# Gated attention with a hash-routed expert layer: blocks of three sizes, gating of two groups on TensorE, u loads on another queue

## The chip, the cores and the metric

One core of one Trainium2 chip runs the whole program. The metric is the device time of one execution in microseconds. The kernel before was timed three times; the median counts. Engines are named as the profile names them: PE (TensorE matmul), PEld (its weight loads), DVE (VectorE), ACT (ScalarE), POOL (GpSimd), SP (SyncE).

## What is computed

Attention without softmax, multiplied by a gate, and then a layer of 8 experts in which an integer hash of the token's id picks the one expert of each token. All in fp32.

```python
# u, v: (8, 2496, 256)   z: (8, 2496, 64)
scores = (1.0 / S) * np.matmul(z, z.transpose(0, 2, 1))
attn = np.maximum(scores, 0.0) ** 2
x = (u * np.matmul(attn, v)).reshape(8 * 2496, 256)
# w1: (8, 256, 1024)   w2: (8, 1024, 256)
expert_idx = token_ids * np.int64(2654435761) % np.int64(8)
for e in range(8):
    m = expert_idx == e
    out[m] = np.maximum(x[m] @ w1[e], 0.0) @ w2[e]
```

## The kernel before

The program has two stages that TensorE goes through one after the other, attention and experts. The order of the work on every engine is the order in which the code emits it: a manual schedule is entered before the first load and left at the end, so what stands first on an engine's queue is done first, and an instruction that waits holds up all behind it on the same engine or DMA queue. Tiles rotate through pools of fixed numbers of buffers.

*Products.* Both stages multiply 2x2 block matrices with seven block products in place of eight (a Winograd form). It costs sums of blocks on VectorE: in attention `sums` (L258, four subtractions on the scores, L261 to L264) and `join` (L313, ACT copy L320 and DVE L322 to L328, which read the accumulators); in the experts the subtractions in `turn_x` and four operations on the hidden blocks (L912 to L915). The generator `products` (L860) emits one of the seven products at each `next`, in the order 1, 6, 7, 5, 2, 3, 4, and the operations that combine them behind them: L864 (ACT copy), L866, L871, L872, and L879 and L882 for the last ones. Product 3 accumulates into the PSUM bank of product 5, which L872 reads first.

*Attention.* Eight batches, each with five groups of queries `g`, each with five steps over keys: 200 steps. A step takes scores on TensorE (`score`, product L228), squares and clips them on ACT and DVE (L242 to L250), takes sums, and accumulates on TensorE (`attend`, L301, product L310). Scores are symmetric, so some are turned by DVE (L272), kept in HBM (L281) and read back (L289). z is read in pieces, turned by DVE (L171) from `zn` tiles. The group's last step is followed by `join`.

*Gating and sorting.* The joined outputs `o` have queries along the free dimension. For all groups but the last, `gate` (L330) turns them on DVE, `put` (L347) writes them to HBM, `fetch` (L353) reads them back by rows into `x_row` and loads u (`load_u`, L202, issued on SP's queue, L206), `multiply` (L370, DVE L374) multiplies by u, and `sort` (L390, GpSimd's indirect DMA L395) scatters the rows to the slots of their experts in HBM. For the last group `gate_late` (L376) turns the outputs by TensorE with an identity (L384), multiplies straight from PSUM (L386) and sorts; it is spread over the first expert step.

*Routing.* A generator (L415 to L604), advanced once per attention step from the sixth on, computes each token's expert and slot. In it DVE counts the tokens (`have`, L488), and after a `yield` a small matmul (L492) adds the counts over partitions. Another generator prepares sums of weights in HBM (`prepare`, L627, sums L644 and L645).

*Experts.* The slots form blocks of one expert each: NL=32 large ones of 512 slots and NR=35 small ones of 128, which hold what large ones leave. A large block goes through `load_x` (L679, SP), `turn_x` (L686, DVE transposes L697, subtractions L702 to L705), `up_large` (L886; product L901 of 4 instructions of 256 columns; 7 products in each of two halves of the hidden width), ACT activations L908, and `down_large` (L917; product L931 of 16 instructions of 128 columns). A small block uses plain products, `up_small` (L946, L954, 32 instructions of 128 columns) and `down_small` (L962, L965, 16 of 256 columns). `store` (L852, L854) scatters the output rows by GpSimd. `load_w` (L712) loads the weights of a block on SP (L717, L720, L724).

The loop L989 has one step for each large block: up products of block i, down products of block i−1, and the turning of block i+1, interleaved by the string ORDER (L976): U and u are up products of a large and a small block, D and d down products, X and x parts of `turn_x`, G parts of `gate_late`. SMALL (L982) spreads the small blocks over the steps, one or two in each. After its step, the x of the blocks of step i+2 and their weights are loaded on SP's queue. The first two blocks are "SURE": their x is loaded ahead, and turned in the last two attention steps.

Of the kernel before, what the change touches and what calls it, by code (L numbers as in the profile page):

```python
# [25 lines left out]
def kernel(  # L26
# [26 lines left out]
    BLK = 512  # L53
    TB = BLK // P
    NL = -(-(N - E * (BLK - 1)) // BLK)
    NR = (N - NL * BLK + E * (P - 1)) // P
    NB = NL + NR
    NS = NL * TB + NR

# [142 lines left out]
    def load_u(b, g, home=None):  # L202
        u_sb[b, g] = (home or rowpool).tile([P, 2, 2, D], F32, name="u_sb")
        for t in range(2):
            n = keys(g, t)
            nc.sync.dma_start(out=u_sb[b, g][0:n, :, t],  # L206
                              in_=uf[ds(b * S, S), :].rearrange("(q s) d -> s q d", q=2)[ds(g * W + t * P, n)])
# [105 lines left out]
    def join(g, acc, home):  # L313

        w = queries(g)
        p = {m: acc[k][:, half, 0:w] for m, (k, half) in BANK.items()}
        o = home.tile([P, DP, 2, W], F32, name="o")
        r = opool.tile([P, 2, W], F32, name="r", bufs=1)
        p1, u2 = r[:, 0, 0:w], r[:, 1, 0:w]
        nc.scalar.copy(p1, p[1])  # L320
        c = lambda i, q: o[:, i, q, 0:w]
        nc.vector.tensor_add(c(0, 0), p1, p[2])  # L322
        nc.vector.tensor_add(u2, p1, p[6])
        nc.vector.tensor_add(c(0, 1), u2, p[5])
        nc.vector.tensor_add(c(0, 1), c(0, 1), p[3])
        nc.vector.tensor_add(u2, u2, p[7])
        nc.vector.tensor_add(c(1, 1), u2, p[5])
        nc.vector.tensor_sub(c(1, 0), u2, p[4])  # L328
        return o
# [46 lines left out]
    def gate_late(b, g, o):  # L376

        x_sb = late.tile([P, 2, 2, D], F32, name="x_row")
        for q in range(2):
            ps = down_ps.tile([P, 2, D], F32, name="g_ps", tag="any")  # L380
            for t in range(2):
                m = keys(g, t)
                for i in range(DP):
                    nc.tensor.transpose(ps[0:m, t, ts(i, P)], o[:, i, q, ds(t * P, m)], ident[:])  # L384
                x, y = times_u(b, g, x_sb, q, t, m)
                nc.vector.tensor_mul(x, ps[0:m, t].rearrange("p (h i k) -> p i h k", h=DP, k=L), y)  # L386
                sort(b, g, x_sb, 2 * q + t)
            yield
# [26 lines left out]
    def places():  # L415

        with tc.tile_pool(name="route", bufs=1) as route:
# [31 lines left out]
            def fill():  # L449
                if unfilled:  # L450
# [3 lines left out]
                        x_dram[ds(NL * BLK + c * P, n * P), :].rearrange("(c p) d -> p c d", p=P), zero[:].unsqueeze(1).to_broadcast([P, n, D]))  # L454
# [35 lines left out]
            yield  # L490
# [23 lines left out]
            upto = wpool.tile([P, E, C], F32, name="upto", tag="w")  # L514
# [10 lines left out]
            nc.vector.tensor_tensor_scan(upto[:].rearrange(flat_e), one[:].to_broadcast([P, E * C]), upto[:].rearrange(flat_e), 0.0,  # L525
                                         op0=OP.mult, op1=OP.add)
            yield
            nc.vector.tensor_add(rank[:], rank[:], upto[:])
# [21 lines left out]

            large, large_end = share(count, BLK, 0, NL, "large")
            in_large = route.tile([P, E], F32)
            nc.vector.tensor_scalar(in_large[:], large[:], float(BLK), None, op0=OP.mult)
            nc.vector.tensor_sub(count[:], count[:], in_large[:])
            small, small_end = share(count, P, P - 1, NR, "small")

            shift = route.tile([P, E], F32)
            nc.vector.tensor_sub(shift[:], large_end[:], large[:])  # L560
            nc.vector.scalar_tensor_tensor(shift[:], shift[:], float(BLK), first[:], op0=OP.mult, op1=OP.subtract)
            more = route.tile([P, E], F32)
            nc.vector.tensor_sub(more[:], small_end[:], small[:])
            nc.vector.tensor_scalar(more[:], more[:], float(P), float(NL * BLK), op0=OP.mult, op1=OP.add)
            nc.vector.tensor_add(first[:], first[:], in_large[:])
            nc.vector.tensor_sub(more[:], more[:], first[:])
            nc.vector.tensor_sub(more[:], more[:], shift[:])

            for end, b0, nb in ((large_end, 0, NL), (small_end, NL, NR)):
# [4 lines left out]
                eb = route.tile([1, max(NL, NR)], F32, name="eb")  # L576
# [9 lines left out]
            past = upto  # L586
            nc.vector.tensor_tensor(past[:], rank[:], each(first), op=OP.is_ge)
            yield
            nc.vector.tensor_mul(past[:], past[:], each(more))
            yield  # L590
            nc.vector.tensor_add(rank[:], rank[:], each(shift))
            yield
            nc.vector.tensor_add(rank[:], rank[:], past[:])
            yield
# [78 lines left out]
    def large(j):  # L673
        return j < NL

    def slot_tiles(j):
        return range(j * TB, (j + 1) * TB) if large(j) else range(NL * (TB - 1) + j, NL * (TB - 1) + j + 1)

    def load_x(j):  # L679
        n = len(slot_tiles(j)) * P  # L680
        xq[j] = gpool.tile([P, n // L, DP, L], F32, name="xq" if large(j) else "xqs")
# [4 lines left out]
    def turn_x(j):  # L686

        n = len(slot_tiles(j))
        if large(j):
            x = gpool.tile([P, 2, DP, 2 * P], F32, name="xT")  # L690
            t = gpool.tile([P, 4, 2 * P], F32, name="xs")
        else:
            x, t = gpool.tile([P, 1, DP, P], F32, name="xTs"), None
        xT[j] = x, t
        m = min(2, n) * P // L
# [12 lines left out]
    def turn_x_at_once(j):  # L708
        for _ in turn_x(j):
            pass  # L710

    def load_w(j, m):  # L712

        e = nc.sync.value_load(eb_i[0:1, j:j + 1], min_val=0, max_val=E - 1)
        if large(j):
# [13 lines left out]
    order.__enter__()  # L729

# [42 lines left out]
    for i, (b, g, s) in enumerate(steps):  # L773
# [14 lines left out]
        if i >= len(steps) - SURE:  # L788
            turn_x_at_once(i - len(steps) + SURE)
        if pos == NT - 1:  # L790
            done = (b, g, join(g, acc, opool if i < len(steps) - 1 else late))
# [8 lines left out]
        if pos == 0 and done is not None:  # L800
# [19 lines left out]
        elif is_routed:  # L820
# [6 lines left out]
            if len(fetched) < 2 and waiting and (len(waiting) > 1 or i > put_at + (1 if i < len(steps) - NT else 0)):  # L827
# [9 lines left out]
        if i == len(steps) - 2:  # L837
            load_u(b, g, late)
            load_w(1, 0)
# [46 lines left out]
    def up_large(j):  # L886
# [3 lines left out]
        h = hpool.tile([P, 2, 2, FQ, 2 * P], F32, name="h")  # L890
        sums = hpool.tile([P, 3, FQ, 2 * P], F32, name="hs")
        hid[j] = h, sums
        take = {1: (0, y11), 2: (2, y21), 3: (6, y22), 4: (3, t4), 5: (4, t1), 6: (5, t2), 7: (1, t3)}
        for f in range(0, FQ, 2):
            def made(m, ps):
                first = ps is None
                if first:
                    ps = up_ps.tile([P, 2, 2 * P], F32, name="h_ps", tag="held" if m in (1, 5) else "other")
# [5 lines left out]
            r = rpool.tile([P, 2, 2, 2 * P], F32, name="r")  # L904
# [12 lines left out]
    def down_large(j):  # L917
        h, sums = hid[j]
        x11, x12, x21, x22 = (h[:, k, i] for i in range(2) for k in range(2))
# [3 lines left out]
        def made(m, ps):  # L923
            first = ps is None
            if first:
                held = m in (1, 5)
                ps = down_ps.tile([P, 2, P], F32, name="o_ps", tag="held" if held else "other", bufs=2 if held else 1)
            x, k = take[m]
            for t in range(2):
# [4 lines left out]
        r = rpool.tile([P, 2, 2, P], F32, name="ro")  # L934
        o = rpool.tile([P, TB, D], F32, name="o_sb")
        c = lambda i, k: o[:, ts(i, 2), ts(k, P)]

        def done(x, i, k, ps=None):
            if ps is not None:
                nc.scalar.copy(x, ps)  # L940
            elif i != k:
                for t in (2 * i, 2 * i + 1):
# [19 lines left out]
    def down_small(j):  # L962
        ps = down_ps.tile([P, D], F32, name="o_ps", tag="any")
        for f in range(FP):
# [10 lines left out]

    ORDER = {"": "UuUDUuUDUdUDU" "XUDXUDUxUDUUDU", "made": "UuUDUuUDUdUDU" "XUDXuUDUxuUDUUDU",  # L976
             "next": "UuUDUuUDUdUDU" "XUDXUDUxUDUUxDU", "last": "UdUDUuUDUuUDU" "XUDXUDdUxUDUUDU",
             "first": "UUUUGUUGUUUUUUUU", "second": "DUDUUDUUDUUDUU" "xXUuDUXUuDUxUU"}
# [3 lines left out]
    SMALL = [range(0)] + [range(*(NL + (k * NR + NL // 2) // (NL - 1) for k in (i, i + 1))) for i in range(NL - 1)]  # L982
    assert all(1 <= len(x) <= 2 for x in SMALL[1:]) and max(len(x) for x in SMALL[1:4]) == 1 and SMALL[-1][-1] == NB - 1

    def at(i):

        return [i, *SMALL[i]] if 0 <= i < NL else []

    for i in range(NL + 1):  # L989
        parts = {}  # L990
        for j in at(i):
            parts.setdefault("U" if large(j) else "u", []).append((up_large if large(j) else up_small)(j))
        for j in at(i - 1):
            parts.setdefault("D" if large(j) else "d", []).append((down_large if large(j) else down_small)(j))
        for j in at(i + 1):
            if j >= SURE:
                parts.setdefault("X" if large(j) else "x", []).append(turn_x(j))
        if i == 0:
            parts = {"U": parts["U"], "G": [gate_late(*done)]}
        if i == 1:  # L1000
            parts["x"].insert(0, turn_x(SMALL[1][0]))
        parts = {p: chain(*x) for p, x in parts.items()}
        for p in ORDER["first" if i == 0 else "second" if i == 1 else next((k for k, n in (("made", i), ("next", i + 1), ("last", i - 1)) if len(at(n)) > 2), "")]:
# [3 lines left out]
        if i == 0:  # L1007
            closing["late"].close()
            w2pool = pool("w2pool", 2, reuse_waits="tile")
            load_w(0, 1)  # L1010
            for j in SMALL[1]:
                load_w(j, 0)
                load_x(j)
        for j in at(i + 2):
            load_x(j)
        for m in range(2):
            for j in at(i + 2 - m)[:2]:
                load_w(j, m)
        for m in range(2):
            for j in at(i + 2 - m)[2:]:  # L1020
# [31 lines left out]
```

## Time and profile before

| what | value |
|---|---|
| runs, us | 2515.74, 2511.03, 2512.28; median 2512.28 |
| profiled execution, us | 2507.8 |
| its span from first to last instruction, us | 2506.0 |
| granted TensorE clock, mean | 0.998 |
| ACT activations of scores, L242 | 508, 248.1 us in all |
| products L310 | 42% of the chain that ended last |
| products L931, L901, L228, L954, L965 | 16%, 15%, 8%, 5%, 5% of that chain |
| DMA moved | 557.19 MB, mean 222 GB/s |
| w loads, 1792 KB each, to landing | 11.3 us |
| u loads, 256 KB a group, to landing | 5.2 us |

All times are of one profiled execution, except the runs. A timeline line gives start, duration, engine, code line, operation, written and read tiles with their shape, and how many instructions are taken together; in brackets stands how long the engine idled before it and what released it. A line of waits gives engine, tile and line that waited, what for, then total, number of times and longest. A line of windows gives a stretch, its length, and busy time (number of instructions) of PE, PEld, DVE, ACT and POOL, then the granted clock, the share of the DMA engines and GB/s. [...]

### The profile page before, as it was taken

The numbers are of one execution on the slowest core, as the hardware profiler recorded it, in microseconds if no ns is written. First come the engines' busy times: TensorE is split into PE (matmuls) and PEld (weight loads), VectorE is DVE, ScalarE is ACT, GpSimd is POOL, SyncE is SP. The second block draws the span as 40 slices with busy tenths as digits, with TensorE's granted clock in tenths as the row PEclk, the third lists the DMA queues.
The fourth block names the chain that finished last, engine by engine and source line by source line (L and its number), as shares of the span: only waits on it lengthen the run. The fifth ranks groups of instructions, "written<-read, shape, count | busy, mean of one in ns | idle before, by whom it ended". The sixth has DMA issues, their size and how long they took to land.

```text
span 2506.0 us, 36968 instructions
## 1 busy us (share of the span) xinstructions
PE 2476.4 (99%) x13631; PEld 2110.9 (84%) x13631; DVE 1653.4 (66%) x3151; ACT 705.8 (28%) x1203; POOL 548.9 (22%) x532
## 2 busy tenths in 40 slices
PE   8999999999999999999999989999999999999998
PEld 6787787787787777877787889999999999999998
DVE  7798768768778677687687665545555555555553
ACT  4324324224223233133233112222222222222221
POOL 0000333322332233233223221111111111111112
PEclk9999999999999999999999999999999999999999
DMA  8776899798797897897888797766676667667762
GB/s 148 201 206 176 244 272 227 211 248 203 234 262 191 244 249 184 251 250 198 246 244 230 200 284 240 244 227 227 236 236 203 222 225 232 204 224 245 236 217 72
DMA packets 604661, 557.19 MB, mean 222 GB/s; under 512 B 287068, under 2 KB 544685, under 8 KB 594240
## 3 DMA queue, kind: packets, MB, share of 16 engines
q1 hardware_dynamic: 513984, 369.74, 54.6%
q10 hardware_dynamic: 63168, 97.86, 11.9%
q0 software_dynamic: 27328, 87.23, 10.0%
q8 instruction: 107, 1.75, 0.3%
q14 instruction: 74, 0.61, 0.1%
HBM read 375.55 MB, written 175.60 MB: 220 GB/s over the span
## 4 chain that ended last, share of the span: by engine, by line
PE 91%; DMA 5%; DVE 2%; issue 1%; SPq 0%; ACT 0%; POOL 0%; POOLq 0%; DVEq 0%; ACTq 0%
PE acc L310 42%; PE o_ps L931 16%; PE h_ps L901 15%; PE s_ps L228 8%; PE h_ps L954 5%; PE o_ps L965 5%; DMA a<-scores 3%; DMA u_sb<-in_u_dram 1%; DMA scores<-mirror 0%; DMA zn<-in_z_dram 0%; DVE x_row L374 0%; DVE t L261 0%; DVE t L262 0%; DVE t L263 0%; ACT a L242 0%
## 5 line engine op out<-in xcount | busy, mean ns | idle before, releaser
L242 ACT ACTIVATE a<-s_ps 128x512 f32<-128x512 f32 (+2 forms) x508 | 248.1, 579 | 736.5 <-PE s_ps L228 697.5
L310 PE MATMUL acc<-t,vc 128*128 128x256 f32 (+3 forms) x1600 | 402.6, 374 | 0.0
L310 PEld LDWEIGHTS acc<-a,v_sb 128*128 128x128 f32 (+1 forms) x1600 | 293.3, 190 | 125.0 <-issue 45.5
L310 PE MATMUL acc<-a,v_sb 128*128 128x256 f32 (+3 forms) x1600 | 382.6, 382 | 5.3 <-DVE o L322 5.2
L395 POOL DMA_INDIRECT x_slots<-x_row,row x160 | 192.3, 1202 | 849.7 <-DVE x_row L374 642.9
L310 PE MATMUL acc<-t,v_sb 128*128 128x256 f32 (+3 forms) x1600 | 369.7, 373 | 0.0
L310 PEld LDWEIGHTS acc<-t,vc 128*128 128x128 f32 (+1 forms) x1600 | 303.0, 190 | 34.5
L310 PEld LDWEIGHTS acc<-t,v_sb 128*128 128x128 f32 (+1 forms) x1600 | 303.5, 190 | 33.6
L261 DVE TENSOR_TENSOR t<-a 128x512 f32<-128x512 f32 (+1 forms) x200 | 134.5, 672 | 226.5 <-ACT a L250 162.0
L901 PE MATMUL h_ps<-xs,w 128*128 128x256 f32 x1024 | 258.1, 380 | 0.0
L931 PEld LDWEIGHTS o_ps<-w,h 128*128 128x128 f32 x2048 | 248.6, 192 | 6.5
L228 PE MATMUL s_ps<-zT 64*128 64x512 f32 (+1 forms) x960 | 241.4, 617 | 9.1 <-DVE zT L171 8.4
L931 PE MATMUL o_ps<-w,h 128*128 128x128 f32 x2048 | 249.3, 275 | 0.0
L908 ACT ACTIVATE h<-h 128x512 f32<-128x512 f32 x192 | 121.0, 630 | 349.1 <-DVE h L872 153.2
L854 POOL DMA_INDIRECT out_dram<-o_sb,idx x128 | 126.7, 990 | 420.8 <-ACT h L908 271.2
L272 DVE STREAM_TRANSPOSE mirror<-a 128x512 f32<-128x512 f32 x320 | 198.4, 677 | 6.6 <-DMA scores<-mirror 6.5
L310 PE MATMUL acc<-a,vc 128*128 128x256 f32 (+3 forms) x800 | 201.1, 374 | 0.0
L901 PE MATMUL h_ps<-xT,w 128*128 128x256 f32 x768 | 194.0, 382 | 1.2 <-DVE h L872 1.2
L901 PEld LDWEIGHTS h_ps<-xs,w 128*128 128x128 f32 x1024 | 178.5, 191 | 15.5
L931 PEld LDWEIGHTS o_ps<-w,hs 128*128 128x128 f32 x1536 | 186.4, 192 | 4.8
L931 PE MATMUL o_ps<-w,hs 128*128 128x128 f32 x1536 | 187.1, 275 | 0.0
L611 POOL DMA_INDIRECT slot_tokens<-token,addr x160 | 169.7, 1061 | 49.0 <-issue 48.1
(154 smaller groups left out, 2756.7 us busy)
## 6 DMA issues: line engine op xcount, KB each, us to landing
w<-w_blocks SPq DMA_DIRECT2D x64, 1792.0 KB, 11.3
scores<-mirror SPq DMA_DIRECT2D x276, 256.0 KB, 4.8
a<-scores ACTq DMA_DIRECT2D x48, 1024.0 KB, 5.8
w1s<-in_moe_w_dram SPq DMA_DIRECT2D x35, 1024.0 KB, 10.3
w2s<-in_moe_w_dram SPq DMA_DIRECT2D x35, 1024.0 KB, 11.5
a<-scores ACTq DMA_DIRECT2D x32, 896.0 KB, 7.3
w_blocks<-w POOLq DMA_DIRECT2D x16, 1792.0 KB, 8.1
u_sb<-in_u_dram SPq DMA_DIRECT2D x72, 256.0 KB, 5.2
```

The lines of the kernel that those rows point to most:

```text
L228: nc.tensor.matmul(to, z_h[:, ds(h * HS + s * W + j * P, P)], at, start=True, stop=True)
L242: nc.scalar.activation(to, at, AF.Relu, scale=1.0 / S)
L261: nc.vector.tensor_sub(t1, y12, y11)
L272: nc.vector.transpose(m[:, :, j, h].rearrange("p (n i) k -> p i n k", i=QB), a[:, j, h].rearrange("p (i t) q r -> p i (t q) r", t=2))
L310: nc.tensor.matmul(acc[k][:, half, 0:w], x[0:n, j, :], y[0:n, j], start=(first and j == 0 and half == 0), stop=(last and j == 1), skip_gro ...
L395: st = nc.gpsimd.indirect_dma_start(out=x_dram[:, :], out_offset=bass.IndirectOffsetOnAxis(ap=row[0:m, c:c + 1], axis=0), in_=x_sb[0:m, q, ...
L611: st = nc.gpsimd.indirect_dma_start(out=slot_dram[:, None], out_offset=bass.IndirectOffsetOnAxis(ap=addr[0:n, to:to + 1], axis=0), in_=tok ...
L854: st = nc.gpsimd.indirect_dma_start(out=out[:], out_offset=bass.IndirectOffsetOnAxis(ap=idx[:, col:col + 1], axis=0), in_=o, in_offset=Non ...
L901: nc.tensor.matmul(ps[:, r], w1[j][:, k, ts(f + r, P)], y, start=first and r == 0, stop=True, skip_group_check=True)
L931: nc.tensor.matmul(ps[:, t], x[:, f, ts(t, P)], w2_block(w2[j], k)[:, f], start=first and t == 0 and f == 0, stop=f == FQ - 1, skip_group_ ...
L954: nc.tensor.matmul(ps[:, i, :], w1[j][:, c, ts(f + i, P)], x[:, 0, c, 0:P], start=(c == 0), stop=(c == DP - 1))
L965: nc.tensor.matmul(ps[:], hid[j][:, f], w2[j][:, f, :], start=(f == 0), stop=(f == FP - 1))
```

## The change

1. Blocks come in three sizes: NL=32 of 512, NM=7 of 256 (mid), NR=21 of 128. Mid blocks use the seven products with operands of half the size (`up_big`, `down_big`), so their up products have 4 instructions of 128 columns and their down products 8. They stand at positions 4, 9, 14, 19, 24, 29 and 34 of 39 big blocks. A step has at most one small block; seven of them are put into the step after a mid, the others into other steps. The step loop has 39 steps and an end of down products with the last small one last.
2. Routing computes shares for three sizes, with one more comparison and multiplication on VectorE; the `yield` between `have` and the count matmul is gone.
3. `load_u` issues on GpSimd's queue. The last group's u is loaded four attention steps before the end, that of the group before it (group 3) in that group's last step.
4. The outputs of group 3 of the last batch, like those of the last group, are turned by TensorE and multiplied from PSUM (`gate_at_once`), in the fourth step from the end; they don't go through HBM.
5. In the first expert step both halves of the last group are turned behind the fourth up product into the two "held" banks of `down_ps`; multiplications and sorts are emitted behind all fourteen up products.
6. The two SURE blocks are turned one attention step earlier.
7. Twelve products of the identity with itself stand first on TensorE.

```diff
-            nc.sync.dma_start(out=u_sb[b, g][0:n, :, t],
+            nc.gpsimd.dma_start(out=u_sb[b, g][0:n, :, t],
...
-    def gate_late(b, g, o):
-        x_sb = late.tile([P, 2, 2, D], F32, name="x_row")
+    def gate_at_once(b, g, o, x_sb, bank):
+        made = []
         for q in range(2):
-            ps = down_ps.tile([P, 2, D], F32, name="g_ps", tag="any")
+            made.append(bank())
+            for t in range(2):
+                for i in range(DP):
+                    nc.tensor.transpose(made[q][0:keys(g, t), t, ts(i, P)], o[:, i, q, ds(t * P, keys(g, t))], ident[:])
+        yield
+        for q in range(2):
             for t in range(2):
                 m = keys(g, t)
-                for i in range(DP):
-                    nc.tensor.transpose(ps[0:m, t, ts(i, P)], o[:, i, q, ds(t * P, m)], ident[:])
                 x, y = times_u(b, g, x_sb, q, t, m)
-                nc.vector.tensor_mul(x, ps[0:m, t].rearrange("p (h i k) -> p i h k", h=DP, k=L), y)
-                sort(b, g, x_sb, 2 * q + t)
-            yield
+                nc.vector.tensor_mul(x, made[q][0:m, t].rearrange("p (h i k) -> p i h k", h=DP, k=L), y)
...
                 nc.vector.tensor_reduce(have[:], mask[:], axis=AX.X, op=OP.add)
             fill()
-            yield
             ps = mm_ps.tile([P, E], F32, name="cnt_ps", tag="mm")
             nc.tensor.matmul(ps[:], all1[:], have[:], start=True, stop=True)
...
+    warm = mm_ps.tile([P, P], F32, name="warm", tag="mm")
+    for _ in range(12):
+        nc.tensor.matmul(warm[:], ident[:], ident[:], start=True, stop=True)
...
-        if i >= len(steps) - SURE:
-            turn_x_at_once(i - len(steps) + SURE)
+        if i == len(steps) - 4:
+            x_sb = rowpool.tile([P, 2, 2, D], F32, name="x_row", bufs=3)
+            for _ in gate_at_once(*done, x_sb, lambda: mm_ps.tile([P, 2, D], F32, name="g_ps", tag="mm")):
+                pass
+            to_sort += [(*done[:2], x_sb, k) for k in range(4)]
+        if 0 <= i - (len(steps) - 3) < SURE:
+            for _ in turn_x(i - (len(steps) - 3)):
+                pass
...
         if i == len(steps) - 2:
-            load_u(b, g, late)
             load_w(1, 0)
+        if i == len(steps) - NT - 1:
+            load_u(b, g)
+        if i == len(steps) - 4:
+            load_u(b, g, late)
...
-    def up_large(j):
+    def up_big(j):
+        n = half(j)
-        h = hpool.tile([P, 2, 2, FQ, 2 * P], F32, name="h")
+        h = hpool.tile([P, 2, 2, FQ, 2 * P], F32, name="h")[:, :, :, :, 0:n]
...
-    def down_large(j):
+    def down_big(j):
+        n = half(j) // P
-            for t in range(2):
+            for t in range(n):
...
-    ORDER = {"": "UuUDUuUDUdUDU" "XUDXUDUxUDUUDU", "made": "UuUDUuUDUdUDU" "XUDXuUDUxuUDUUDU",
-             "next": "UuUDUuUDUdUDU" "XUDXUDUxUDUUxDU", "last": "UdUDUuUDUuUDU" "XUDXUDdUxUDUUDU",
-             "first": "UUUUGUUGUUUUUUUU", "second": "DUDUUDUUDUUDUU" "xXUuDUXUuDUxUU"}
+    ORDER = {"first": "UUUUGUUUUUUUUUU", "second": "DUDUDUUDUUDUU" "XUxUDUXUDUUUU",
+             "other": "UuUDUuUDUdUDU" "XUDXUDUxUDUUDU", "end": "DDDDDDDd"}
...
+    for i in range(NBIG):
+        BIG.append(mid.pop(0) if i % (NBIG // NM) == NBIG // NM - 1 and mid else large.pop(0))
+        SMALL.append([])
+    for behind in (True, False):
+        for i in range(NBIG - 1, 1, -1):
+            if small and BIG[i] < NL and (BIG[i - 1] >= NL) == behind and (behind or i % 2 == 0 or len(small) == 1):
+                SMALL[i].append(small.pop())
...
+            parts["G"] = gate_at_once(*done, x_sb, lambda: down_ps.tile([P, 2, D], F32, name="g_ps", tag="held", bufs=2))
...
         if i == 0:
+            for k in range(4):
+                sort(*done[:2], x_sb, k)
```

## The prediction, made before the changed kernel ran

> **What bounds the kernel now.** I read the page's busy times first, then what TensorE waits for, then windows and timelines around each edit.
>
> ```profile
> PE 2476.4 (99%) x13631; PEld 2110.9 (84%) x13631; DVE 1653.4 (66%) x3151; ACT 705.8 (28%) x1203; POOL 548.9 (22%) x532
> ...
> PE s_ps L228 <- DVE zT L171: 8.4, 2, 7.3
> PE g_ps L384 <- DVE x_row L386: 5.6, 2, 4.7
> PE acc L310 <- DVE o L322: 5.2, 7, 1.9
> PE h_ps L901 <- DVE h L872: 1.2, 1, 1.2
> ...
> 1520.00:2480.00 960.00, 960.00 (x6562) 903.52 (x6561) 508.27 (x920) 228.33 (x422) 148.91 (x152) 1.00 0.68 221
> ```
>
> TensorE is busy for 2476.4 of 2506.0 us, at a granted clock of 0.998. Its waits (total, times, longest) add up to about 21 us, and in the expert stage from 1520 to 2480 us it has none. So the change pays where it removes matmul time or one of these few waits, and costs where it makes a new one. The danger is VectorE's queue; this is the second half of an expert step, where TensorE never waits now:
>
> ```profile
> 1917.04 0.69 DVE L882 TENSOR_TENSOR h<-h,h_ps 128x512 f32<-128x512 f32 x1 [1.96 <-PE h_ps L901]
> 1917.64 1.30 DVE L697 STREAM_TRANSPOSE xT<-xq 128x512 f32<-128x512 f32 x2
> ...
> 1923.86 1.95 PE L931 MATMUL o_ps<-w,hs 128*128 128x128 f32 x16
> 1924.28 0.44 DVE L697 STREAM_TRANSPOSE xTs<-xqs 128x256 f32<-128x256 f32 x1
> 1924.64 0.65 DVE L871 TENSOR_TENSOR h<-r,h_ps 128x512 f32<-128x512 f32 x1
> 1925.40 0.69 DVE L872 TENSOR_TENSOR h<-h,h_ps 128x512 f32<-128x512 f32 x1
> 1925.65 1.89 PE L901 MATMUL h_ps<-xT,w 128*128 128x256 f32 x8
> ```
>
> From the end of the first half's 7th up product (1916.83) VectorE works without a gap until L872 ends at 1926.09. The sixth up product of the half accumulates into the bank that L872 reads; it is the second half of the x8 row, so it starts at 1925.65 + 0.86 = 1926.51. The slack is 0.42 us.
>
> [...] the first 16 score products take 6.08 us, later ones 1.99 for 8, that is 3.98 for 16. [...]
>
> **Part by part.** Pace on TensorE: 16 products of 128 columns start 1.787 us after 16 others (2492.36 to 2494.15), 0.1117 each; 4 of 256 columns take 0.864, 0.216 each.
>
> (1) *Blocks.* A large block is 14 up products of 4 instructions of 256 columns (14×0.864 = 12.1) and 7 down products of 16 of 128 columns (7×1.787 = 12.5), 24.6 in all. A small one is 32×0.1117 + 16×0.216 = 7.03. Check: between the small down products at 1649.79 and 1681.41 lie one of each, 31.62. A mid block has 56 up and 56 down instructions, all of 128 columns, 112×0.1117 = 12.51, and stands for two small ones, 14.06 (35 small become 21 and 7 mid). Gain 1.55×7 = −10.85. That gain is on the bounding engine, so it shows unless something stalls it.
>
> (2) *VectorE behind a mid block.* In the step behind a mid, the down products are the mid's: 8 instructions, 0.894 us instead of 1.787. Three come before the sixth up product, so TensorE arrives 3×0.893 = 2.68 earlier: 9.68−2.68 = 7.0 us after the half begins. VectorE's chain shrinks only in two combines of the down products (0.42 to 0.29 each): 9.26−0.26 = 9.0. Where no small block follows in the next step, its transpose and pitch go (−0.35): 8.65. Stalls 2.0 in four steps and 1.65 in three: 4×2.0+3×1.65 = +13.0. It can't fall below nothing, since a wait gives no time back; above, the pitch between operations, of which this step has some that no row shows at 128 columns, could add 1 us. In the mid's own step (up products small, its down products large) chain and TensorE are 7.2 to 7.4 against 7.6: no stall, but slack of only 0.15 to 0.3. The same count applied to the first expert step gives 1.15 where the trace shows the 1.18 wait at 1474.21, which is why I believe it.
>
> (3) *Count wait.* The removed yield puts the count matmul of routing directly behind the reduction L488, on TensorE ahead of the next scores:
>
> ```profile
> 92.66 1.99 PE L228 MATMUL s_ps<-zT 64*128 64x512 f32 x8
> ...
> 94.27 1.48 DVE L488 TENSOR_REDUCE have<-mask 128x8 bf16<-128x1280 bf16 x1
> ```
>
> TensorE would be ready at 92.6, the reduction ends at 95.75: +3.2 (2.4 to 3.5). Behind the waiting matmul stand the scores and all of the next attention step. The 0.76 wait of L310 for L328 goes into it.
>
> (4) *First expert step.* Now 22.1 us from 1453.93 to the first down product at 1476.04: 12.1 of up products, 1.6 of transposes with their gaps, and stalls of 4.71, 1.64 (8 up products at 1462.78 take 3.53 instead of 1.89), 0.90 and 1.18. After: the transposes go to two banks of their own without waiting, the pure up chain still stalls (1.15), and the first down product needs a held bank that the gate multiplies read; on VectorE these multiplies stand behind the last up product's subtraction (0.69) and four sums (4×0.62), and the first bank takes two of them (0.84): 4.2 with the hand-over. That makes 12.1+1.1+1.15+4.2 = 18.55, so −3.55. Were the bank free at once it would be −7.7; the worst is 0. Four sorts on GpSimd follow (1.27 apart, row L854's pitch); the load of block 2's x waits for them, and weights are queued behind it on SyncE: they land about 1.5 us before use, taken as hidden. If not, up to +3.
>
> (5) *Group 3 by TensorE too.* Eight transposes are added to attention, +1.1 with the change of bank; its four VectorE multiplies and the missing round trip through HBM are hidden under 99% busy TensorE.
>
> (6) *u by GpSimd.* 80 issues of under 1 us on an engine 22% busy are hidden; they stand before sorts there, which are not waited for until the expert stage. Four of the seven L310<-L322 waits (0.78, 0.89, 0.42, 0.20) come after VectorE waited for u, which in all waits 22.5 us for it. −2.0 (0 to −2.3).
>
> (7) *Start.*
>
> ```profile
> 7.26 6.08 PE L228 MATMUL s_ps<-zT 64*128 64x512 f32 x16 [7.26 <-DVE zT L171]
> 14.47 2.78 PE L228 MATMUL s_ps<-zT 64*128 64x512 f32 x8 [1.14 <-DVE zT L171]
> ```
>
> [...] up to 2.1 in the first row and 0.8 in the second. But the third score needs key rows that land only at about 13.1, so most turns into waiting: −1.0 (−0.3 to −2.2).
>
> (8) *End.* TensorE ends at about 2497.6; four stores follow on GpSimd, 1.27 apart, and the span ends 8.3 later. With a small down product last, one store follows, end about 6.15 after: −2.1; the large products before it lose their filler, and the third waits for its single bank: +0.7. Net −1.4. (9) Small orders and VectorE's third routing level: +0.5, between 0 and +2, since the level's operations (some 20 short ones) meet a VectorE that is two thirds busy.
>
> Sum: −10.85 +13.0 +3.2 −3.55 +1.1 −2.0 −1.0 −1.4 +0.5 = −1.0. Against the profiled execution (2507.8, its span 2506.0) that is 2506.8. That run lies 4.5 below the median of the three timed ones, 2512.28 (2511.03 to 2515.74); applied to the median, 2511.3.
>
> **Rivals.** *Faster:* the VectorE chain doesn't delay TensorE behind mids, because its operations start earlier than my count (for: 508 of 960 us busy only; against: no gap in the 9 us shown). Without the 13.0 it is −14.0: 2498.3. It decides once the stalls fall under 9 us, 1.3 a mid. *Slower:* the chain is a little longer than counted, in the mid's own step and behind it; slack 0.15 to 0.3 there is thin. With 1 us more behind, and 0.85 in the mid's step: 7×1.85 = 13, so 2524; it passes the bound from about 0.85 us a mid. For: the 128-wide price is an estimate and VectorE works in program order; against: the check in (2) hits 0.03. *Not doing what it says:* a 128-column product at 0.1117 is 52% of a 256-column one, already counted, so mids do save. *Late weights:* a mid step lasts about 19 us, and 1520 to 2480 moves 221 GB/s at 0.68 share; 4.7 MB in 19 us is 250, so priced at nothing.
>
> **Numbers.** A measurement can tell 0.2%, 5.0 us, from no change: faster below 2507.3, slower above 2517.3. My forecast 2511.3, own range 2507 to 2517: 0.44. Faster rival 0.35, 2495 to 2507; slower rival 0.21, 2517 to 2526. The range, 2496 to 2525, takes in most of both.
>
> **What would show it.** Right: about seven waits of 1.7 to 2 us of the sixth up product on L872's successor behind each mid; a wait near 95 us of about 3; one of about 4 ahead of the first down product; fewer L310<-L322 waits; one store at the end. Wrong: no TensorE wait behind mids (faster), or waits also in the mids' own steps, for weights or x (slower).

## The result and the profile after

The changed kernel takes 2529.01 us (median of 4 runs, 2526.24 to 2530.63), the kernel before 2513.51 beside it (2511.03 to 2515.74). The ratio is 1.0061, with an interval of 1.0043 to 1.0078: some 15 us slower, where 2511.3 was forecast and 2525 was the end of the range. The profiled execution took 2530.63 us, its span is 2528.9.

These are the changed kernel's busy times from the page, and then what TensorE waited for (total, times, longest). Line numbers are those of the changed file: L900 is L872 of before, L325 is L322, L930 and L961 are the products L901 and L931, L312 is L310, and L492 and L495 are the reduction L488 and the count matmul L492. The waits for the join are those of a query group's first product for L325, which reads the accumulators of the group before.

```profile
PE 2481.5 (98%) x13775; PEld 2116.0 (84%) x13775; DVE 1715.7 (68%) x3346; ACT 722.8 (29%) x1259; POOL 604.8 (24%) x612
...
PE h_ps L930 <- DVE h L900: 13.2, 8, 1.9
PE acc L312 <- DVE o L325: 12.5, 5, 3.8
PE o_ps L961 <- DVE x_row L392: 4.0, 1, 4.0
PE cnt_ps L495 <- DVE have L492: 3.2, 1, 3.2
```

Three of these four came close to the forecast: the queue behind mid blocks (8 waits, one of them the 1.18 of the first expert step), the gate multiplications (4.0 of 4.2), and the count (3.2 of 3.2). The second was not: waits for the join were to fall by 2, and rose from 5.2 to 12.5. And the first line has a puzzle. TensorE should have 10.85 us less to do and is busy for 5.1 us more. The windows of the changed kernel show most of the reason. The column behind the five busy times (PE, PEld, DVE, ACT, POOL, each with its count) is the granted clock:

```profile
14.40:21.00 6.60, 6.60 (x13) 3.55 (x14) 6.50 (x15) 5.31 (x8) 0.00 (x0) 0.50 0.63 190
99.70:103.00 3.30, 3.30 (x9) 1.85 (x6) 0.00 (x0) 3.00 (x6) 0.00 (x0) 0.50 0.89 293
325.00:328.20 3.20, 3.20 (x9) 2.52 (x8) 3.13 (x8) 0.00 (x0) 0.25 (x1) 0.50 0.97 314
577.60:584.20 6.60, 5.79 (x14) 4.62 (x15) 6.46 (x16) 0.66 (x1) 5.08 (x6) 0.50 0.63 190
1492.40:1495.60 3.20, 3.20 (x13) 2.84 (x13) 0.00 (x0) 0.37 (x1) 2.59 (x3) 0.50 0.35 113
```

In five places TensorE runs at half its clock. The stretches of 0.50 in this trace are 3.4 us long or twice that, 23.9 us in all. Where TensorE works through one, it loses half of it, 1.7 or 3.4 us; for all five that makes some 11 us. Before, there was one such stretch behind the start:

```profile
1462.80:1466.00 3.20, 3.20 (x9) 2.57 (x9) 0.42 (x1) 0.60 (x1) 2.41 (x3) 0.50 1.00 417
```

Step by step, profiled execution against profiled execution (spans 2528.9 and 2506.0, +22.9), read from the starts of the same products in both timelines. Starts are used since rows overlap: four products take 1.03 us as a row and start 0.864 us apart.

| step of the prediction | forecast | measured |
|---|---|---|
| (7) start: score product at 23.42, now 25.73 | −1.0 | +2.3 |
| (3) count wait: 3.3 at once, 5.3 with the low clock, of which 1.2 come back by 139 us | +3.2 | +4.1 |
| (9) third routing level: wait of 2.20 for the join at 175.57 | +0.5 | +2.2 |
| joins from 300 to 600 us: waits of 3.85, 2.31 and 3.42 (2.4 in all before), low clock after two | 0 | +11.9 |
| (6) u's waits in later batches | −2.0 | −2.7 |
| (5) group 3's transposes | +1.1 | +0.9 |
| (4) first expert step: 22.11, now 18.55; then the low clock | −3.55 | −3.6 and +1.7 |
| (1) block shape, by the count of products and their pace | −10.85 | −10.9 |
| (2) VectorE behind mids: seven losses of 1.78 to 2.02 | +13.0 | +13.1 |
| (8) end: from TensorE's last product to the last store | −1.4 | −2.1 +0.6 |
| end: from the last store to the span's end | 0 | +4.1 |

The lines sum to 21.6; 1.3 us are not assigned. The profiles differ by more than the medians (15.5). One reason is that before's profiled run was faster than the four beside which the changed kernel was timed (2507.8 against 2511.03 to 2515.74). The other is the line of the joins, which holds for this one execution: the wait of 3.42 us at 578.41, with 2.8 us lost to the low clock behind it, is 0.97 without a low clock in the profile of run 4 below, whose attention is the same code. There the line is +3.8. With 3.8 in place of 11.9 the lines sum to 13.5.

### The profile page after: what moved, and what is told of

Its sections match the earlier page's. It is cut to its first block, busy times and chain, and to the rows that moved or that the text cites. A ratio compares the mean times of both kernels' runs of the same rounds, so it can differ in the third digit from the quotient of the medians.

```text
span 2528.9 us, 37390 instructions
## 1 busy us (share of the span) xinstructions
PE 2481.5 (98%) x13775; PEld 2116.0 (84%) x13775; DVE 1715.7 (68%) x3346; ACT 722.8 (29%) x1259; POOL 604.8 (24%) x612
## 3 DMA queue, kind: packets, MB, share of 16 engines
q10 hardware_dynamic: 63168, 97.86, 11.9%
## 4 chain that ended last, share of the span: by engine, by line
PE 89%; DVE 4%; DMA 4%; issue 1%; ACT 0%; SPq 0%; ACTq 0%; POOL 0%; DVEq 0%; POOLq 0%
PE acc L312 43%; PE o_ps L961 16%; PE h_ps L930 15%; PE s_ps L230 8%; PE h_ps L984 3%; PE o_ps L995 3%; DMA a<-scores 2%; DMA xq<-x_slots 1%; DMA zn<-in_z_dram 1%; DVE t L263 0%; ACT a L244 0%; DVE xT L714 0%; DVE t L265 0%; DVE t L264 0%; DVE h L900 0%
## 5 line engine op out<-in xcount | busy, mean ns | idle before, releaser
L312 PEld LDWEIGHTS acc<-a,v_sb 128*128 128x128 f32 (+1 forms) x1600 | 297.0, 192 | 134.9 <-issue 52.3
L312 PE MATMUL acc<-t,vc 128*128 128x256 f32 (+3 forms) x1600 | 403.6, 374 | 0.0
L312 PE MATMUL acc<-a,v_sb 128*128 128x256 f32 (+3 forms) x1600 | 388.6, 386 | 12.5 <-DVE o L325 12.5
L312 PE MATMUL acc<-t,v_sb 128*128 128x256 f32 (+3 forms) x1600 | 369.7, 373 | 0.0
L312 PEld LDWEIGHTS acc<-t,vc 128*128 128x128 f32 (+1 forms) x1600 | 304.4, 190 | 34.4
L312 PEld LDWEIGHTS acc<-t,v_sb 128*128 128x128 f32 (+1 forms) x1600 | 303.4, 190 | 33.6
L882 POOL DMA_INDIRECT out_dram<-o_sb,idx x142 | 140.1, 987 | 638.8 <-ACT h L937 437.7
L930 PE MATMUL h_ps<-xs,w 128*128 128x256 f32 (+1 forms) x1248 | 287.8, 361 | 0.0
L961 PEld LDWEIGHTS o_ps<-w,h 128*128 128x128 f32 x2272 | 276.3, 192 | 11.6 <-DVE x_row L392 4.4
L961 PE MATMUL o_ps<-w,h 128*128 128x128 f32 x2272 | 279.9, 275 | 4.6 <-DVE x_row L392 4.0
L937 ACT ACTIVATE h<-h 128x512 f32<-128x512 f32 (+1 forms) x234 | 138.5, 592 | 395.7 <-DVE h L900 180.3
L930 PE MATMUL h_ps<-xT,w 128*128 128x256 f32 (+1 forms) x936 | 216.6, 363 | 13.2 <-DVE h L900 13.2
L930 PEld LDWEIGHTS h_ps<-xs,w 128*128 128x128 f32 x1248 | 208.0, 191 | 16.3
L961 PEld LDWEIGHTS o_ps<-w,hs 128*128 128x128 f32 x1704 | 206.5, 192 | 6.4 <-DVE o_sb L900 1.8
L961 PE MATMUL o_ps<-w,hs 128*128 128x128 f32 x1704 | 210.1, 275 | 0.0
L312 PE MATMUL acc<-a,vc 128*128 128x256 f32 (+3 forms) x800 | 201.5, 374 | 0.0
L930 PEld LDWEIGHTS h_ps<-xT,w 128*128 128x128 f32 x936 | 162.5, 191 | 32.8 <-DVE h L900 16.4
```

What stands on the lines that cost most here:

```text
L312: nc.tensor.matmul(acc[k][:, half, 0:w], x[0:n, j, :], y[0:n, j], start=(first and j == 0 and half == 0), stop=(last and j == 1), skip_gro ...
L882: st = nc.gpsimd.indirect_dma_start(out=out[:], out_offset=bass.IndirectOffsetOnAxis(ap=idx[:, col:col + 1], axis=0), in_=o, in_offset=Non ...
L930: nc.tensor.matmul(ps[:, r], w1[j][:, k, ts(f + r, P)], y, start=first and r == 0, stop=True, skip_group_check=True)
L937: lambda o, i, k, ps=None: nc.scalar.activation(o, o if ps is None else ps, AF.Relu))
L961: nc.tensor.matmul(ps[:, t], x[:, f, ts(t, P)], w2_block(w2[j], k)[:, f], start=first and t == 0 and f == 0, stop=f == FQ - 1, skip_group_ ...
```

## The experiments

The first kernels test a new theory, that a wait of TensorE has a second price, the low clock behind it, and each part alone. All ratios are against the kernel before on the same chip.

**1. The yield alone.**

```diff
             fill()
-            yield
             ps = mm_ps.tile([P, E], F32, name="cnt_ps", tag="mm")
```

> The kernel before with only the routing yield taken out, so that the count matmul stands directly behind the reduction. Theory (a wait also costs clock): TensorE waits about 3.2 us for the reduction near 95 us, and the granted clock is 0.5 for one stretch of 3.4 us soon after, which costs 1.7 us more: 4.9 us later from there on, and +5 us at the end if the routing, which now ends one attention step earlier, changes nothing else. Rival (a wait costs its length): no stretch of low clock, +3.2 us.

Ratio 1.0021 (1.0010 to 1.0032), 5.2 us. The interval, 2.5 to 8 us, doesn't separate the theory's 5 from the rival's 3.2; the timeline of this kernel's TensorE does:

```profile
95.94 0.17 PE L491 MATMUL cnt_ps<-have,all 128*128 128x8 bf16 x1 [3.16 <-DVE have L488]
96.04 2.54 PE L228 MATMUL s_ps<-zT 64*128 64x512 f32 x8
98.50 3.09 PE L310 MATMUL acc<-a,v_sb 128*128 128x256 f32 x8
```

Eight accumulations take 3.09 where 1.99 is usual, and the granted clock is 0.50 from 97.3 to 100.8 us. The next row starts at 101.43, 5.0 us later than before (96.41), as the theory had it.

**2. u on GpSimd alone.**

```diff
-            nc.sync.dma_start(out=u_sb[b, g][0:n, :, t],
+            nc.gpsimd.dma_start(out=u_sb[b, g][0:n, :, t],
```

> The kernel before with only the loads of u issued on GpSimd's queue. Theory (u without SyncE's queue ahead of it meets the puts and the reads of kept scores and makes these late): waits of 3 to 4 us of the first product of a query group for the join, near 310 and 560 us, each followed by a low clock, +6 to +12 us. Rival (the prediction's step): four of the seven short waits go, -2 us, and the long waits in the changed kernel come from the routing, whose steps end at another attention step.

Ratio 1.0052 (1.0035 to 1.0069). But the cost does not lie where the theory had it. The wait near 310 us is 2.26, that near 560 is 0.73, neither is followed by a low clock, and the join's waits are 4.9 in all, against 5.2. Two other places pay: the last group's u stands behind GpSimd's queue, so that the gate transposes wait 11.7 us instead of 4.7 (with 13.7 us of low clock instead of 3.4, most of it within the wait), which the changed kernel avoids by loading it earlier; and GpSimd ends later. Its last store starts at 2508.09 and the span ends at 2517.05, 9.0 later; before it was 2501.15 and 2506.03, 4.9. The two places make up the whole 11.0 us between the profiles.

**3. The identity products alone.**

```diff
+    warm = mm_ps.tile([P, P], F32, name="warm", tag="mm")
+    for _ in range(12):
+        nc.tensor.matmul(warm[:], ident[:], ident[:], start=True, stop=True)
```

> The kernel before with only the twelve identity products first. Theory[...]: the granted clock falls to 0.5 from about 14 to 21 us as in the changed kernel, and the first accumulation ends 2 us later than without. Rival (the low stretch there is chance of one execution, and the warm products help): clock 1.0 from 14 us on, 1 to 1.6 us earlier.

Ratio 1.0004 (0.9995 to 1.0013). The low clock comes, from 14.5 to 21.3 us, and the scores of 92.66 us come 2.2 later. The total doesn't show it. Of the six kernels that begin with these products and were profiled here, only that of run 6 escaped the low clock; its second score product starts at 22.47 instead of 23.42, just the 1.0 that was forecast.

**4. VectorE's order behind a mid block.**

```diff
+             "behind": "UuUDUuUDUdUDU" "XUDUDUUDXUxUDU"}
...
-        for p in ORDER["first" if i == 0 else "second" if i == 1 else "end" if i == NBIG else "other"]:
+        for p in ORDER["first" if i == 0 else "second" if i == 1 else "end" if i == NBIG else "behind" if BIG[i - 1] >= NL else "other"]:
```

> The changed kernel with another order in the steps behind a mid block: the second part of the turning of the next block, and the turning of the small one, stand behind the fifth down product, not ahead of it. Theory (VectorE's queue is what delays the sixth up product behind mids): the seven waits for h L900, 12.0 us, go, and the kernel is 12 us faster than the changed one. Rival (TensorE waits for something else that comes last at the same time, or the moved operations delay the next step's first products): under 4 us of it comes out.

Ratio 1.0033 (1.0022 to 1.0045), against the changed kernel's 1.0061: some 7 us by the runs, with wide intervals, where 12 were expected. In the profile the waits for h L900 went as the theory says, from 13.2 us to 2.6, and the time from the first down product to the last from 1027.2 to 1016.3. The sixth up product behind the first mid, in the changed kernel and then in this one:

```profile
1618.10 1.03 PE L930 MATMUL h_ps<-xT,w 128*128 128x256 f32 x4
1620.88 1.13 PE L930 MATMUL h_ps<-xT,w 128*128 128x256 f32 x4 [1.76 <-DVE h L900]
```

```profile
1613.10 1.03 PE L930 MATMUL h_ps<-xT,w 128*128 128x256 f32 x4
1614.29 1.13 PE L930 MATMUL h_ps<-xT,w 128*128 128x256 f32 x4 [0.16 <-DVE h L900]
```

From start to start there are 2.78 us in the changed kernel, 1.92 more than the 0.864 of four products; the forecast stall was 2.0. (The wait that the trace names, 1.76, is shorter than what the step loses.) With the turning moved the loss is 0.33.

**5. and 6. One part undone: u, then the yield.**

```diff
-            nc.gpsimd.dma_start(out=u_sb[b, g][0:n, :, t],
+            nc.sync.dma_start(out=u_sb[b, g][0:n, :, t],
```

> The changed kernel with only the loads of u back on SyncE's queue. Theory (u on GpSimd costs twice: GpSimd's last drain ends 8.9 us after the last store's start rather than 4.8, and u's transfers are no longer held back behind the puts, so that the kept scores land late near 317 us): the end is 4.1 us shorter behind the last store, the wait of 3 to 4 us near 324 us and its low clock go, about 9 us faster than the changed kernel. Rival (the wait near 324 us comes from the routing, which ends one attention step later and shifts puts and reads of rows against the kept scores): only the 4.1 us at the end come back.

```diff
             fill()
+            yield
             ps = mm_ps.tile([P, E], F32, name="cnt_ps", tag="mm")
```

> The changed kernel with only the routing yield put back. Theory (a wait costs its length and the clock): the wait of 3.2 us near 98 us and the low clock behind it go, 5 to 6.6 us faster there. If the wait near 324 us depends on the attention step in which routing ends, it changes or goes too, since routing ends one more step later; if it comes from u's loads, it stays at 3 to 4 us.

Ratios 1.0060 (1.0043 to 1.0076) and 1.0068 (1.0047 to 1.0088): neither can be told from the changed kernel's 1.0061 by time, though 9 and 5 to 6.6 us were expected. In their profiles some of the expected pieces moved. With u on SyncE the last store and the span's end (2519.4) are 4.9 us apart; in the changed kernel it is 9.0. The last stores, changed kernel and run 5:

```profile
2519.90 0.97 POOL L882 DMA_INDIRECT out_dram<-o,idx  x1 [0.30 <-issue]
```

```profile
2514.52 0.97 POOL L882 DMA_INDIRECT out_dram<-o,idx  x1 [0.30 <-issue]
```

But a long wait for the join stays, at another place: 3.85 us at 359.95 in run 5. So such a wait comes without u's loads on GpSimd too, and my theory of u's transfers fell. In run 6 the count wait and its low clock are gone, and waits of 1.41 and 2.29 with a low clock stand at 381 to 386 us, and one of 3.19 at 1291. Both have the routing later than before, run 5 by one attention step and run 6 by two: its third level brought two yields more, and taking out the count's yield took one back.

**7. and 8. The blocks with their cover.**

```diff
 run 7: u on SyncE, the yield back, no identity products, "behind" as in run 4
 run 8, beside that:
-    ORDER = {"first": "UUUUGUUUUUUUUUU",
+    ORDER = {"first": "UUUUGUUUUUUUUUGU",
```

> The changed kernel with u on SyncE, the yield back, no identity products first, and the turning moved in the steps behind mid blocks. Theory (the block shape saves its 10.85 us of products, and what takes the gain away is the waits that the other parts and VectorE's queue make): against the kernel before -10.85 for the blocks, +1 for what stays of the waits behind mids, -3.6 in the first expert step with +0 of clock, +1.1 for group 3, -1.5 at the end, +2 for the wait near 176 us: about -12, 0.5% faster. Rival (the blocks save less, for example since a product of 128 columns with other weight loads costs more beside them): within 0.2% of the kernel before.

> The kernel of the run before this one with the gate multiplications of the last group ahead of the fourteenth up product of the first expert step, not behind all. Theory: the first down product no longer waits 4.0 us for them, and TensorE's clock, which falls for 3.4 us or more there, stays: 4 to 6 us faster than that kernel. Rival (the multiplications delay the last up product's operations on VectorE by as much, 1.7 us, and another wait takes the place): 0 to 2 us faster.

Run 7 has 1.0003 (0.9995 to 1.0012), not −12 us. Attention ends at 1463.31 us, 9.4 later than before, of which 3.1 were expected; the first expert step is 2.9 shorter; from the first to the last down product 1016.3 us pass instead of 1021.6, with a low clock (1.7) in them that the sum of the expectation left out; and the end is 2.1 shorter. So blocks, first step and end save 10.2 us of the 15 expected, and attention takes nearly all of it away, in waits for the join of 11.2 us where before has 5.2:

```profile
PE acc L312 <- DVE o L325: 11.2, 9, 2.9
```

Run 8 has 0.9982 (0.9975 to 0.9989), 5.3 us faster than run 7 and as much as expected: the wait of 4.0 of the first down product is 0.6, and the low clock behind it is gone.

**9., 10. and 12. When sorting starts.** The routing is moved by two attention steps: later in the kernel before, earlier in the kernel of run 8 and in the changed kernel.

```diff
 run 9 (on before):
             for _ in range(2):
                 yield
                 fill()
             yield
+            yield
+            yield
 runs 10 (on run 8) and 12 (on the changed kernel):
             for _ in range(2):
-                yield
                 fill()
             yield
```

> The kernel before with two more yields at the start of the routing, so that all of it, and with it sorting and reading back of rows, comes two attention steps later, and nothing is added. Theory (the step at which sorting starts makes the waits for the join between 310 and 400 us in all kernels with three block sizes, by gathering puts, reads and scatters on the DMA engines): such waits grow from 1.9 us in the kernel before to 4 us or more, and the kernel is 3 to 6 us slower. Rival (u's queue or VectorE's third routing level makes them): they stay under 3 us, and the time within 0.1%.

> The fastest kernel so far (u on SyncE, the yield back, no identity products, turning moved behind mids, gate multiplications early) with the routing two attention steps earlier, by dropping two of the yields that only spread its start. Theory (the step at which sorting starts makes the waits): those between 310 and 400 us, 8.5 us in that kernel's profile, fall to 3 us or less, about 5 us faster. Rival: they stay, within 0.1%.

> The changed kernel with only the routing two attention steps earlier (the two yields dropped that spread its start). Theory (the step at which routing ends and sorting starts makes most of the extra waits in attention): the waits for the join between 170 and 600 us, 11.8 us in four places with two low clocks in the changed kernel's profile, fall to 4 us or less, and the kernel is 8 to 15 us faster than the changed one; u's end of 8.9 us behind the last store's start stays. Rival (u's loads on GpSimd make them): they stay at 8 us or more, and the time within 4 us.

Run 9: 1.0013 (1.0006 to 1.0021), 3.3 us slower, of 3 to 6 expected. Nothing but the step of routing differs, and waits for the join of 0.80, 2.95 and 2.09 with a low clock stand at 311 to 388 us, where before has one of 1.92.

Run 10: 0.9935 (0.9919 to 0.9952), 16 us faster than before; the join's waits are 1.7 in all instead of 11.5. By the ratios it is about 12 us faster than run 8, by the spans 6.5; some 5 were expected.

Run 12: 1.0043 (1.0027 to 1.0058), 4.5 us better than the changed kernel by the ratios, whose intervals overlap, and 11.5 by the spans; 8 to 15 were expected. Its waits for the join are 3.7, of which 0.2 lies between 100 and 600 us, while the count's grew:

```profile
PE cnt_ps L494 <- DVE have L491: 4.0, 1, 4.0
...
PE acc L312 <- DVE o L325: 3.7, 3, 2.3
```

The waits for the join between 300 and 600 us, before and in runs 9, 8 and 10 in this order:

```profile
PE acc L310 <- DVE o L322: 2.4, 2, 1.9
PE acc L310 <- DVE o L322: 6.4, 4, 2.9
PE acc L312 <- DVE o L325: 7.1, 3, 2.8
PE acc L312 <- DVE o L325: 0.8, 1, 0.8
```

All fourteen profiles fall into the same two groups. Where the routing is one or two steps later than before (the changed kernel, runs 4 to 9), these waits are 4.3 to 9.6 us in all; where it is at the same step or one earlier (before, runs 1, 2, 3, 10, 11 and 12), 0.2 to 3.4. Each group has kernels with u on either queue, and kernels with two and with three block sizes.

In run 12 the 2.2 us wait near 170 us is gone too. In the changed kernel VectorE works there through L537 to L592, two bursts of some 5 us of short operations (155.5 to 160.9 and 163.4 to 168.4) in place of one of 6.8 before, and the join stands behind them; in run 12 the join stands ahead of them. How far the step of routing makes the waits near 320 through the DMA engines was not measured apart. What the changed kernel's trace shows is that VectorE waited for kept scores there, and so came late to the join. Such a wait alone is not enough: before has a longer one between 300 and 400 us, of 12.0, and no join waits more than 1.92 there.

```profile
316.97 0.69 DVE L263 TENSOR_TENSOR t<-a 128x512 f32<-128x512 f32 x1 [8.50 <-DMA a<-scores]
...
324.03 0.37 DVE L325 TENSOR_TENSOR o<-r,acc 128x256 f32<-128x256 f32 x1
```

**11. The wait of run 1, filled with work.**

```diff
             fill()
-            yield
-            ps = mm_ps.tile([P, E], F32, name="cnt_ps", tag="mm")
+            cnt = mm_ps.tile([P, P], F32, name="cnt_ps", tag="mm")
+            for _ in range(12):
+                nc.tensor.matmul(cnt[:], ident[:], ident[:], start=True, stop=True)
+            ps = cnt[:, 0:E]
```

> The kernel before without the routing yield, as in the first run, with twelve identity products in the bank of the count, ahead of the count matmul: TensorE works for 2.7 us of the 3.2 us that it waited. Theory (the idle time itself takes the clock away): no stretch of low clock near 97 us, and the scores behind come 3.2 us later than in the kernel before instead of 4.9. Rival (something else lowers the clock there, such as the switch to the bf16 count matmul): the low clock stays.

The timeline, to be laid beside run 1's:

```profile
92.41 2.84 PE L492 MATMUL cnt_ps<-ident 128*128 128x128 f32 x24
95.64 0.17 PE L494 MATMUL cnt_ps<-have,all 128*128 128x8 bf16 x1 [0.39 <-DVE have L488]
95.74 1.99 PE L228 MATMUL s_ps<-zT 64*128 64x512 f32 x8
97.65 1.99 PE L310 MATMUL acc<-a,v_sb 128*128 128x256 f32 x8
```

The granted clock (third number from the end) from 97.4 to 100.7 us, in run 1 and in this one:

```profile
97.40:100.70 3.30, 3.30 (x9) 1.84 (x6) 0.00 (x0) 2.96 (x6) 0.00 (x0) 0.50 0.74 259
97.40:100.70 3.30, 3.30 (x16) 2.71 (x15) 0.00 (x0) 3.27 (x6) 0.00 (x0) 1.00 0.79 274
```

The next row of accumulations starts at 99.48 instead of 101.43: 1.95 us from useless products. So here the idle time takes the clock, not the change to bf16; the kernel before has the same bf16 matmul, without a wait, and no low clock behind it. All five profiles with this wait unfilled have one. The whole, 1.0008 (0.9999 to 1.0017), is 3.3 us below run 1, though the intervals overlap.

## Why the prediction was wrong, step by step

By the medians the forecast was missed by 16.5 us (−1.0 forecast, 15.5 measured). What failed are the terms for the start (7, +2.3 for −1.0), for the end (6 and 8, 4.1 more than counted) and for the routing (9, whose joins were put at nothing and cost 11.9 in the profile, 3.8 in that of run 4), and the half clock behind waits, 1.7 us a stretch, which no term had.

**Steps 1, 2, 4 and 5 held in their lengths.** VectorE's queue took 13.1 of 13.0 forecast, 1.9 to 2.0 us in four steps and 1.8 in three, and the operations of 128 columns, put at 0.29, took 0.28 to 0.29; in the trace of before those of 512 columns take 0.69, of 256 0.42, and the 128-column ones of L198 to L200 0.285 to 0.292. The block shape saved 10.9 of 10.85. The first down product came 18.55 us after attention's end, the forecast to the hundredth, which is partly luck: the wait in it is 3.98 of 4.2. The likeliest case, that mids gain and lose about the same, was right.

**Step 3 failed in its price.** "TensorE would be ready at 92.6, the reduction ends at 95.75: +3.2" is the wait. The half clock behind it, 1.7 us or more, was left out, and so it was behind the wait of step 4. My sum had a slower pace at the start alone. The trace of before had shown one behind a wait, too. Step 4 counts "stalls of 4.71, 1.64 (8 up products at 1462.78 take 3.53 instead of 1.89)"; the second of these is no stall, but the low clock after the first (0.50 from 1462.80 to 1466.00 us, above). In the profiles here all 22 waits of 3.0 us or more after the start have one or more such stretches at or behind their end. Those of 2.0 to 3.0 us have one in 6 of 20 cases, and in run 10 there is one behind a wait of 1.67 and one behind 1.86. So a wait under 3.0 us is not safe from it here. Which of the shorter waits are hit is open: that of 2.15 near 169 us is hit in run 8 and not in run 6.

**Step 6 missed where u's move costs.** "Hidden" was said of 80 issues, 0.71 to 0.93 us each in the changed kernel, on an engine 22% busy. GpSimd's end, 4.1 us later in each of the five profiled kernels that load u there and in none of the other nine, is on the path. The gain of 2 us in the later batches came (2.7), but not surely by u's move: run 3, with u on SyncE, gains 1.3 over the same stretch.

**Step 7 had the wrong sign.** Its 2.1 and 0.8 us were my estimate of what work ahead could save, the 6.08 and 2.78 of the first two rows less the 3.98 and 1.99 of later ones. The 24 products end at 6.9 us, and the first sixteen scores behind them are faster (4.47 for 6.08, at a granted clock of 1.00 in both; the cause was not shown), but the clock is lost at 14.3 us, behind two waits for the key rows, and the accumulations run at half rate: +2.3 where −1.0 was forecast. Why it is lost after waits of 1.1 and 0.3 us, and not in run 6, is open.

**Step 9 and what wasn't in the sum.** "+0.5, between 0 and +2" was for VectorE's third level, which cost 2.2. That the level's yields end the routing one attention step later, and so move the start of sorting for the whole of batch 1, was not counted. Its line is the largest of the table, though how large changes from one execution to the next. Run 9 shows it with the step alone changed, and runs 10 and 12 from the other side; by what path a later start delays the joins is open. **Step 8** had the store right (−2.1), and the end of GpSimd was not in it.

The result lies past the slower rival's range too, and by another mechanism: that rival had VectorE late in the mid's own step, and no such wait appears.

## What to carry to other kernels

Price a wait of TensorE of three microseconds twice: its length, and the clock behind it, 1.7 us a stretch, which came with all 22 waits of 3.0 us or more here. Products without use in the wait can get the second part back, as they did in run 11 (1.95 us); at the start they lost the clock in five of six profiles. A generator that is advanced once a step is a clock for everything that starts at its end: a yield added or taken away shifts that start, and can cost more than the operations at the yield.

The fastest version (run 10) has u on SyncE, no identity products, the turning and gate multiplications moved, and the routing two steps earlier, at before's step: 2497.25 us against 2511.57 beside it.

## What was not expected of the hardware

Loading u through GpSimd lengthens the time from the last store's start to the end of the span from 4.9 to 9.0 us, the same in five profiles, although the last such load lies 1000 us earlier. Why GpSimd ends these 4.1 us later was not measured.
